# Backward pass of one decode step: two heads' M kept in PSUM, part of wq kept on chip, another order in the third pass

## The chip, the cores and the metric

The kernel runs on one core of a Trainium2 chip. The metric is the device time of one execution in microseconds; the time before is the median of three runs. A profiled execution, recorded apart from those runs, gives the trace. The engines are TensorE (PE, with PEld for its weight loads), VectorE (DVE), ScalarE (ACT), GpSimd (POOL) and SyncE (SP). DMAs are issued by ScalarE, GpSimd and SyncE, each on a queue of its own, and all run on the same 16 DMA engines.

## The reference

The forward pass is one token through attention over a cached window and a gated feed-forward layer; what is asked for is its output and the gradients of everything that goes in:

```python
W = min(4096, max(256, Sk // 4))                      # 4096 of Sk = 32768
q = (layernorm(x) @ wq)                               # 16 heads of 256, 8 K/V heads
scores = einsum("bhqd,bhkd->bhqk", q, k[last W]) * (Dh ** -0.5)
p = softmax(scores); o = einsum("bhqk,bhkd->bhqd", p, v[last W])
h  = x + o @ wo
h2 = h + ((hn @ w_gate) * (hn @ w_up)) @ w_down       # hn = layernorm(h)
_out, _vjp = jax.vjp(_f, x, k_cache, v_cache, wq, wo, w_gate, w_up, w_down)
return (_out, *_vjp(grad_out))
```

All tensors are bf16. x and grad_out have 448 numbers, wq is 448x4096, wo 4096x448, w_gate and w_up 448x1792, w_down 1792x448, and each cache 8 heads x 32768 x 256. The gradients of the two caches (out_2, out_3) are zero outside the last 4096 positions of each head: 28,672 of 32,768 rows of 256 numbers, 235 MB in all, are zeros to be written. The gradient of wq is out_4, of wo out_5, of w_gate and w_up out_6 and out_7, of w_down out_8; out_0 is h2 and out_1 the gradient of x.

## The kernel before

The kernel has a first pass over the 8 K/V heads (forward attention), a middle part (feed-forward, forward and backward, and the gradient of the attention output), and a third pass over the heads, which writes the cache gradients. A scheduler orders the instructions of each engine at build time; each engine then works through its own list in that order and waits where an operand isn't there.

**On-chip memory.** One arena, laid out by hand: offsets are in KB per partition (KB = 512 bf16 elements). S1 to S4 hold 16 KB each, MB is a region of 32 KB, RB one of 52.5 KB, and there are two buffers outside, `home` (16 KB) and `pair` (32 KB). V_of and K_of say where the V and K of each head lie. V of heads 5 and 6 lies in the halves of `pair`, V of head 7 in S2.

**Zero fills.** The zeros of the 16 regions go out on SyncE's queue, issued at L248. Two early ones read a cleared `pair`; the others read 32 cleared rows of `home`, at most two in flight (DEEP). One of them (UNEVEN) is cut into unequal parts.

**First pass** (`scores`, `moments`, the loop over g in which `scores(g+1)` is called before `moments(g)`). For each head, `dots` transposes K on TensorE (L311) and multiplies it with q (L314); after the softmax, `moments` scales K by the probabilities on VectorE (L367) and accumulates on TensorE M, the product of V and the scaled K (L371), and the sums for o (L375). M (128 x 1024 f32 in two PSUM banks) is copied by ScalarE to M_sb (L379), in MB. The first loads are all on SyncE's queue (L121, L122, L209); later K and V are loaded on ScalarE's queue when `NEXT` says, after the head whose slot they take. MB holds wq (wqA 24 KB, wqB 4 KB) until q is computed (L231, L233). K of head 3 is loaded into MB, after that.

**Middle.** wo (L398, L402), w_down (L399) and the gate and up weights (L404, L405) are loaded into RB and beyond. The gradient for o comes from 32 dot products of wo with dh on VectorE (L509) and a product (L514).

**Third pass**, in the head order 3, 1, 4, 5, 0, 6, 2, 7. For each head, `dots` again (V with the gradient of o, on TensorE at L311 and L314, copied by VectorE and ScalarE at L655 and L653), then 16 products (L680) whose results VectorE (L687, L688) and ScalarE (L684, L685) cast to two staging buffers (`stage`), and a pair of stores of 2048 KB each on ScalarE's queue (L690). `plan` adds other jobs to each iteration. `dq_all` computes dq from the eight M (L562 to L570), in the first iteration. `spread_all` writes the rows of the gate and up gradients into `pair` (L408, L412, L413). GpSimd computes the weight gradients: `job_d` (out_8), `job_o` (out_5), `job_g` and `job_gB` (out_6, out_7), `job_q` and `job_qB` (out_4), each into one of two staging buffers `wst` of 12 KB (L580, L609 to L612), and stores them on its own queue (L591, L596, L603, L620, L625, L635). For the gradient of x, wq is loaded again into `pair` (L695, L696, L701) and multiplied with dq on VectorE (L707, L710). V of heads 0 and 2 is brought into S3 (L692, L693, and a load at L209).

Of the kernel before, what the change touches and what calls it, by code (L numbers as in the profile page):

```python
# [8 lines left out]
f32 = mybir.dt.float32  # L9
# [4 lines left out]
D = 448  # L14
# [21 lines left out]
def kernel(  # L36
# [20 lines left out]
    def ar(off, n):  # L57
        return arena[:, off:off + n]
# [16 lines left out]
    KT_slot = [ar(RB + (32 + 2 * i) * KB, 2 * KB) for i in range(3)]  # L75
# [132 lines left out]
    def load_kv(dst, cache, g, queue=LD):  # L208
        queue.dma_start(out=dst, in_=cache[0, g, Sk - W:, :].rearrange("(p t) d -> p t d", t=T))  # L209
# [31 lines left out]

    load_kv(K_of[3], A_k_cache, 3, ZQ)

    def rows_of(src, n):
# [76 lines left out]
    with tc.tile_pool(name="ps_m", bufs=1, space=bass.MemoryType.PSUM) as ps_m, \  # L321
            tc.tile_pool(name="ps_x", bufs=1, space=bass.MemoryType.PSUM) as ps_x, \
            tc.tile_pool(name="ps_c", bufs=1, space=bass.MemoryType.PSUM) as ps_c, \
# [35 lines left out]
        def moments(g, p_f):  # L359
            K_sb, V_sb = K_of[g], V_of[g]  # L360
            M_ps = ps_m.tile([128, 2, 2 * Dh], f32, tag="M")
            for c in range(8):
                pK = pK_slot[c % 2]
                for i in range(4):
                    t = 4 * c + i
                    for hh in range(2):
                        nc.vector.tensor_scalar(out=pK[:, i, hh, :], in0=K_sb[:, t, :], scalar1=p_f[:, 8 * i + c, hh:hh + 1], scalar2=None, op0=ALU.mult)  # L367
                for i in range(4):
                    t = 4 * c + i
                    for vh in range(2):  # L370
                        nc.tensor.matmul(M_ps[:, vh, :], lhsT=V_sb[:, t, vh * 128:(vh + 1) * 128], rhs=pK[:, i, :, :].rearrange("p h d -> p (h d)"),  # L371
                                         start=(t == 0), stop=(t == T - 1))
# [41 lines left out]

    with tc.tile_pool(name="ps_mid", bufs=3, space=bass.MemoryType.PSUM) as ps_mid, \
            tc.tile_pool(name="ps_f", bufs=1, space=bass.MemoryType.PSUM) as ps_f, \
            tc.tile_pool(name="workm", bufs=1) as workm:
# [30 lines left out]
        dhn2 = workm.tile([128, 2, 2, 5], f32)  # L448
        ffn_ps = ps_f.tile([1, D], f32, tag="ffn")

# [103 lines left out]
        LD.dma_start(out=out_0.rearrange("a b d -> (a b) d"), in_=h2_bf)  # L554

    with tc.tile_pool(name="work2", bufs=2) as work2, tc.tile_pool(name="lnw", bufs=1) as lnw, \
            tc.tile_pool(name="ps_d", bufs=2, space=bass.MemoryType.PSUM) as ps_d:
# [13 lines left out]

        HJ = H * Dh // 2
        wst_ctr = [0]
# [20 lines left out]
        def job_d(h):  # L594
            def st(buf):
                nc.gpsimd.dma_start(out=out8_v[h], in_=buf[:, 0:NB * D])  # L596
            return lambda: outer([(dh2_bc[:], hh_f[:, h, b:b + 1], D) for b in range(NB)], st)

        def job_g(i):
# [27 lines left out]

        HJ = H * Dh // 2

        def job_qB():  # L630
# [7 lines left out]
        def spread_all():  # L638
            for i in range(2):
                for q in range(4):  # L640
                    spread_dg(diag3, ps_t, "tmp", i, q, dg_bc[:, i, q * D:(q + 1) * D])

        plan = [[dq_all], [job_d(0), job_d(1)], [job_o(0, 13), job_o(13, 13)], [job_o(26, 6), spread_all, job_g(0)], [job_g(1), job_gB()],
                [job_q(0), job_q(1)], [job_q(2), job_qB()], []]

        stc = 0
        for it, g in enumerate((3, 1, 4, 5, 0, 6, 2, 7)):
            V_sb = kv(S[3]) if g in (0, 2) else V_of[g]
# [45 lines left out]
            if it == 3:  # L694
                LD.dma_start(out=wq2A[:, 0, :], in_=wq_A[:, 0, :])  # L695
                LD.dma_start(out=wq2B, in_=wq_B)  # L696
            if it == 4:
                load_kv(kv(S[3]), A_v_cache, 2)
            if it == 5:
                for c in range(1, 3):  # L700
                    LD.dma_start(out=wq2A[:, c, :], in_=wq_A[:, c, :])  # L701
            for job in plan[it]:
                job()
            if it == 6:
                dn1 = lnw.tile([128, 5], f32)
                for c in range(3):
                    nc.vector.tensor_tensor_reduce(out=wq2A[:, c, :], in0=wq2A[:, c, :], in1=dq_bc, scale=1.0, scalar=0.0,  # L707
                                                   op0=ALU.mult, op1=ALU.add, accum_out=dn1[:, c:c + 1])
                for h in range(2):
                    nc.vector.tensor_tensor_reduce(out=wq2A[:, h, 0:HJ], in0=wq2B, in1=dq_bc[:, h * HJ:(h + 1) * HJ], scale=1.0, scalar=0.0,  # L710
                                                   op0=ALU.mult, op1=ALU.add, accum_out=dn1[:, 3 + h:4 + h])
                dcat1 = lnw.tile([128, 8], f32)
# [39 lines left out]
```

## Time and profile before

| what | value |
|---|---|
| time, median of 3 runs | 789.95 us (789.61 to 789.96) |
| the profiled execution's own time | 789.11 us |
| its span, first to last instruction | 787.3 us |
| mean granted TensorE clock | 0.753 |
| TensorE, VectorE, ScalarE, GpSimd busy | 62%, 50%, 25%, 24% of the span |
| HBM read, written | 52.00 MB, 280.59 MB |

The page of the profile cuts the span into 40 slices (19.7 us each) and gives the busy share of each engine in tenths, the DMA engines' mean share and what they moved. Further views are the busy times by stretch, the waits (engine, line, what it waited for, total, times, longest), the chain of work that ended last, and the timeline of single instructions. A name like `arena<-d_ps` is the written tile and the read one.

### The profile page before, as it was taken

What the parts mean: (1) busy time and instruction counts of PE and PEld (TensorE: products, weight loads), DVE (VectorE), ACT (ScalarE), POOL (GpSimd) and SP (SyncE); (2) the same over time, 40 slices, a digit from 0 to 9 for tenths busy, and PEclk for the clock granted to TensorE, in tenths of its full rate; (3) what the DMA queues carried; (4) which work ended last, traced back from release to release, by engine and by line L of the source; (5) the groups of instructions that cost most, each with busy time, mean ns of one, the idle gap of its engine ahead of it and who ended that gap; (6) DMA issues with size and microseconds to landing.
All of it is one profiled execution on the core that took longest, in us unless ns stands there. A gap on an engine that the chain in (4) does not pass through costs nothing.

```text
span 787.3 us, 6396 instructions
## 1 busy us (share of the span) xinstructions
PE 486.3 (62%) x2184; PEld 205.2 (26%) x2184; DVE 396.0 (50%) x1087; ACT 198.0 (25%) x309; POOL 187.0 (24%) x95
## 2 busy tenths in 40 slices
PE   1999999999699929234043156997528605826230
PEld 1444444434344414011012012342212302302000
DVE  8168536436026614213427845267358219897230
ACT  1351331340430001000001025155315302515230
POOL 7000000000000000000000000595934369494710
PEclk9999999999869959565555567998756855556555
DMA  9999999999999999999999999999999999999996
GB/s 379 430 423 432 433 428 422 420 427 431 430 433 429 426 430 429 427 429 428 429 433 432 433 429 420 431 422 428 418 431 420 430 427 432 431 427 420 429 427 282
DMA packets 23118, 333.01 MB, mean 423 GB/s; under 512 B 1290, under 2 KB 2318, under 8 KB 3694
## 3 DMA queue, kind: packets, MB, share of 16 engines
q1 hardware_dynamic: 15189, 255.33, 76.2%
q10 hardware_dynamic: 5320, 56.56, 17.0%
q0 software_dynamic: 2576, 20.71, 6.3%
q8 instruction: 17, 0.28, 0.1%
q14 instruction: 16, 0.12, 0.0%
HBM read 52.00 MB, written 280.59 MB: 422 GB/s over the span
## 4 chain that ended last, share of the span: by engine, by line
PE 47%; DMA 28%; DVE 16%; issue 4%; ACT 2%; SPq 0%; DVEq 0%; ACTq 0%; POOLq 0%
PE M_ps L371 15%; DMA pair<-in_A_wq_dram 8%; DMA arena<-in_B_w_up_dram 8%; PE tr_ps L311 7%; PE rows_ps L314 7%; PE ok_ps L375 6%; DMA arena<-in_A_k_cache_dram 4%; DMA out_dram<-arena 4%; DMA arena<-in_A_v_cache_dram 3%; DVE arena L509 2%; PE d_ps L680 2%; DVE arena L688 2%; DVE arena L687 2%; PE dqb_ps L562 2%; DMA arena<-in_B_w_down_dram 2%
## 5 line engine op out<-in xcount | busy, mean ns | idle before, releaser
L367 DVE TENSOR_SCALAR arena<-arena,p_f 128x256 bf16<-128x256 bf16 x512 | 110.2, 280 | 56.1 <-PE M_ps L371 53.5
L311 PE MATMUL tr_ps<-ident_f,arena 128*128 128x128 f32 x448 | 87.0, 324 | 35.1 <-DMA arena<-in_A_k_cache_dram 21.4
L680 PE MATMUL d_ps<-arena 32*128 32x512 bf16 x256 | 49.4, 515 | 78.5 <-DVE arena L688 67.0
L314 PE MATMUL rows_ps<-arena,vpad 128*16 128x512 bf16 x256 | 89.6, 449 | 9.2 <-ACT arena L653 3.2
L371 PE MATMUL M_ps<-arena 128*128 128x512 bf16 x320 | 78.1, 390 | 16.5 <-DMA arena<-in_A_v_cache_dram 15.2
L328 ACT COPY arena<-tr_ps 128x1024 bf16<-128x1024 bf16 x64 | 63.7, 1013 | 90.3 <-PE tr_ps L311 77.5
L311 PEld LDWEIGHTS tr_ps<-ident_f,arena 128*128 128x128 f32 x448 | 56.4, 161 | 113.8 <-issue 81.0
L687 DVE CAST arena<-d_ps 128x512 bf16<-128x512 f32 x64 | 47.3, 750 | 29.1 <-PE d_ps L680 26.6
L684 ACT CAST arena<-d_ps 128x512 bf16<-128x512 f32 x64 | 38.0, 593 | 93.8 <-PE d_ps L680 87.4
L688 DVE CAST arena<-d_ps 128x512 bf16<-128x512 f32 x64 | 46.8, 742 | 9.5 <-DMA out_dram<-arena 9.5
L653 ACT COPY arena<-tr_ps 128x1024 bf16<-128x1024 bf16 x32 | 32.8, 1028 | 61.8 <-PE rows_ps L314 36.3
L580 POOL TENSOR_SCALAR arena<-dh_bc,oX_f 128x448 bf16<-128x448 bf16 x32 | 44.4, 1398 | 10.8 <-DMA out_dram<-arena 9.9
L371 PEld LDWEIGHTS <-arena 128*128 128x128 bf16 x320 | 30.5, 101 | 53.6 <-DMA arena<-in_A_v_cache_dram 17.3
L375 PE MATMUL ok_ps<-arena 128*32 128x512 bf16 x208 | 43.3, 380 | 0.0
L402 POOL DMA_DIRECT2D arena<-in_A_wo_dram x1 | 0.5, 528 | 179.9 <-PE ok_ps L375 179.9
L685 ACT CAST arena<-d_ps 128x512 bf16<-128x512 f32 x64 | 38.4, 600 | 16.0 <-DMA out_dram<-arena 16.0
L580 POOL TENSOR_SCALAR arena<-pair,xT 128x1792 bf16<-128x1792 bf16 x6 | 35.8, 5978 | 23.4 <-ACT pair L413 23.4
L680 PEld LDWEIGHTS <-arena 32*128 32x128 bf16 x256 | 11.0, 96 | 115.8 <-DVE arena L688 80.2
L707 DVE CUSTOM_DVE_ANT_0 pair<-pair,arena 128x4096 bf16<-128x4096 bf16 x3 | 18.2, 6070 | 40.2 <-DMA pair<-in_A_wq_dram 40.2
L580 POOL TENSOR_SCALAR arena<-arena,xT 128x4096 bf16<-128x4096 bf16 x3 | 31.8, 10612 | 23.3 <-DMA out_dram<-arena 23.3
L379 ACT COPY arena<-M_ps 128x512 f32<-128x512 f32 x16 | 8.6, 589 | 100.4 <-PE M_ps L371 100.4
L316 DVE COPY arena<-rows_ps 16x512 f32<-16x512 f32 x16 | 10.8, 676 | 43.3 <-PE rows_ps L314 43.1
(235 smaller groups left out, 616.0 us busy)
## 6 DMA issues: line engine op xcount, KB each, us to landing
out_dram<-home SPq DMA_DIRECT2D x13, 14336.0 KB, 83.9
out_dram<-arena ACTq DMA_DIRECT2D x16, 2048.0 KB, 25.3
out_dram<-pair SPq DMA_DIRECT2D x2, 14336.0 KB, 79.7
out_dram<-home SPq DMA_DIRECT2D x1, 12288.0 KB
arena<-in_A_k_cache_dram SPq DMA_DIRECT2D x4, 2048.0 KB, 22.0
arena<-in_A_k_cache_dram ACTq DMA_DIRECT2D x4, 2048.0 KB, 20.2
arena<-in_A_v_cache_dram SPq DMA_DIRECT2D x3, 2048.0 KB, 28.4
arena<-in_A_v_cache_dram ACTq DMA_DIRECT2D x3, 2048.0 KB, 24.3
```

The costliest lines, as they stand in the source:

```text
L311: nc.tensor.transpose(tr_ps[:, i, :], X_sb[:, 4 * q + i, :].bitcast(f32), ident_f[:])
L314: nc.tensor.matmul(rows_ps[:], lhsT=pad[:, e, 16 * q:16 * q + 16], rhs=XT.rearrange("p (n e) -> p n e", e=2)[:, :, e], start=(q == 0 and e ...
L328: sT_ps = dots(K_of[g], KT_slot, vpad[g % 2], rows1, ps_c, "cols", lambda q, XT, ps: nc.scalar.copy(out=XT, in_=ps))
L367: nc.vector.tensor_scalar(out=pK[:, i, hh, :], in0=K_sb[:, t, :], scalar1=p_f[:, 8 * i + c, hh:hh + 1], scalar2=None, op0=ALU.mult)
L371: nc.tensor.matmul(M_ps[:, vh, :], lhsT=V_sb[:, t, vh * 128:(vh + 1) * 128], rhs=pK[:, i, :, :].rearrange("p h d -> p (h d)"), start=(t == ...
L375: nc.tensor.matmul(ok_ps[32 * k:32 * (k + 1), :], lhsT=ppad[g % 2][:, t:t + 2, :].rearrange("p t h -> p (t h)"), rhs=X_sb[:, t:t + 2, :].r ...
L580: nc.gpsimd.tensor_scalar(out=buf[:, off:off + n], in0=src, scalar1=col, scalar2=None, op0=ALU.mult)
L680: nc.tensor.matmul(d_ps[:, qi].rearrange("p w d -> p (w d)"), lhsT=rm[32 * q:32 * (q + 1), l, :], rhs=Rs[32 * q:32 * (q + 1), :], start=Tr ...
L684: nc.scalar.copy(out=stV[:, t:t + 2, :], in_=d_ps[:, :, 0, :])
L685: nc.scalar.copy(out=stK[:, t:t + 2, :], in_=d_ps[:, :, 1, :])
L687: nc.vector.tensor_copy(out=stV[:, t:t + 2, :], in_=d_ps[:, :, 0, :])
L688: nc.vector.tensor_copy(out=stK[:, t:t + 2, :], in_=d_ps[:, :, 1, :])
```

## The change

- wqA and wqB lie 4 KB further up in MB, M_sb of heads 6 and 7 lies at RB, and the two `wst` buffers have 8 KB each. So the second half of wq's third block (4 KB) and wqB (4 KB) are not overwritten.
- M of heads 6 and 7 is not copied in the first pass: head 6 stays in its PSUM tile, head 7 is accumulated in the two transpose buffers (`ps_tr`), and both are copied after the wo dots. The pool of M stays open until then; the middle's pool has two banks instead of three, and the feed-forward sum is in the bank of `rows`.
- K of heads 3 to 7 lies in other slots, K of head 3 is loaded on ScalarE's queue after head 0, and `NEXT` has other entries (V of head 7 after head 5 instead of 6).
- `dq_all` is called ahead of the third pass, whose head order is 3, 1, 4, 6, 5, 0, 7, 2.
- The jobs are cut and planned differently; the third row block of out_6 and out_7 has its own job (`job_g2`).
- wq is reloaded as two blocks of 1024 KB and a half of 512 KB, and its dots with dq are one more.

```diff
-    K_of = [kv(o) for o in (RB, RB + 16 * KB, S[4], MB + 16 * KB, RB, RB + 16 * KB, S[2], RB)]
+    K_of = [kv(o) for o in (RB + 16 * KB, RB, S[4], RB + 16 * KB, RB, S[2], RB + 16 * KB, RB)]
-    M_sb = [ar(MB + 4 * KB * g, 4 * KB).bitcast(f32).rearrange("p (v h d) -> p v h d", v=2, h=2) for g in range(G)]
-    wqA = ar(MB, 24 * KB).rearrange("p (c j) -> p c j", c=3)
-    wqB = ar(MB + 24 * KB, 4 * KB)
+    M_sb = [ar(o, 4 * KB).bitcast(f32).rearrange("p (v h d) -> p v h d", v=2, h=2)
+            for o in [MB + 4 * KB * g for g in range(6)] + [RB, RB + 4 * KB]]
+    wqA = ar(MB + 4 * KB, 24 * KB).rearrange("p (c j) -> p c j", c=3)
+    wqB = ar(MB + 28 * KB, 4 * KB)
...
-    dg_bc = pair[:, 0:2 * F].rearrange("p (i f) -> p i f", i=2)
+    dg_bc = pair[:, ZW:ZW + 2 * F].rearrange("p (i f) -> p i f", i=2)
-    wst = [ar(MB + (8 + 12 * i) * KB, 12 * KB) for i in range(2)]
-    wq2A = pair[:, 8 * KB:32 * KB].rearrange("p (c j) -> p c j", c=3)
-    wq2B = ar(P3 + 33 * KB // 2, 4 * KB)
+    wst = [ar(MB + (8 + 8 * i) * KB, 8 * KB) for i in range(2)]
+    HJ = H * Dh // 2
+    wq2 = [pair[:, 0:2 * HJ], pair[:, 2 * HJ:4 * HJ], pair[:, ZW + 4 * KB + 2 * HJ:ZW + 4 * KB + 3 * HJ], wqA[:, 2, HJ:2 * HJ]]
...
-    load_kv(K_of[3], A_k_cache, 3, ZQ)
...
+    def move_M(g, M_ps):
+        for vh in range(2):
+            nc.scalar.copy(out=M_sb[g][:, vh].rearrange("p h d -> p (h d)"), in_=M_ps[vh])
...
-            M_ps = ps_m.tile([128, 2, 2 * Dh], f32, tag="M")
+            if g < G - 1:
+                M_t = ps_m.tile([128, 2, 2 * Dh], f32, tag="M", name="M_t")
+                M_ps = [M_t[:, vh, :] for vh in range(2)]
+            else:
+                M_ps = [ps_tr.tile([128, 4, 128], f32, tag="tr", name="M_t")[:].rearrange("p t k -> p (t k)") for _ in range(2)]
...
-            for vh in range(2):
-                nc.scalar.copy(out=M_sb[g][:, vh].rearrange("p h d -> p (h d)"), in_=M_ps[:, vh, :])
-        NEXT = {0: ((0, 4),), 1: ((0, 5),), 2: ((1, 4), (0, 6)), 4: ((0, 7),), 6: ((1, 7),)}
+            if g < G - 2:
+                move_M(g, M_ps)
+            else:
+                M_late.append((g, M_ps))
+        NEXT = {0: ((0, 3),), 1: ((0, 4),), 2: ((0, 5), (1, 4)), 3: ((0, 6),), 4: ((0, 7),), 5: ((1, 7),)}
...
-    with tc.tile_pool(name="ps_mid", bufs=3, space=bass.MemoryType.PSUM) as ps_mid, \
-            tc.tile_pool(name="ps_f", bufs=1, space=bass.MemoryType.PSUM) as ps_f, \
+    with tc.tile_pool(name="ps_mid", bufs=2, space=bass.MemoryType.PSUM) as ps_mid, \
...
-        ffn_ps = ps_f.tile([1, D], f32, tag="ffn")
+        ffn_ps = ps_s.tile([1, D], f32, tag="rows")
...
+        for g, M_ps in M_late:
+            move_M(g, M_ps)
...
         def job_g(i):
-            ov = (out_6, out_7)[i]
             def st(buf):
-                nc.gpsimd.dma_start(out=ov[0:384, :].rearrange("(p c) f -> p (c f)", c=3), in_=buf[:, 0:3 * F])
-            return lambda: outer([(dg_bc[:, i, :], hnT_f[:, c:c + 1], F) for c in range(3)], st)
+                nc.gpsimd.dma_start(out=out67[i][:, 0:2 * F], in_=buf[:, 0:2 * F])
+            return lambda: outer([(dg_bc[:, i, :], hnT_f[:, c:c + 1], F) for c in range(2)], st)
+        def job_g2():
+            def st(buf):
+                for i in range(2):
+                    nc.gpsimd.dma_start(out=out67[i][:, 2 * F:], in_=buf[:, i * F:(i + 1) * F])
+            return lambda: outer([(dg_bc[:, i, :], hnT_f[:, 2:3], F) for i in range(2)], st)
...
-        plan = [[dq_all], [job_d(0), job_d(1)], [job_o(0, 13), job_o(13, 13)], [job_o(26, 6), spread_all, job_g(0)], [job_g(1), job_gB()],
+        plan = [[job_d(0), job_d(1)], [job_o(0, 9), job_o(9, 9)], [job_o(18, 9), job_o(27, 5)], [spread_all, job_g(0), job_g(1)], [job_g2(), job_gB()],
                 [job_q(0), job_q(1)], [job_q(2), job_qB()], []]
+        dq_all()
-        for it, g in enumerate((3, 1, 4, 5, 0, 6, 2, 7)):
+        for it, g in enumerate((3, 1, 4, 6, 5, 0, 7, 2)):
...
             if it == 3:
-                LD.dma_start(out=wq2A[:, 0, :], in_=wq_A[:, 0, :])
-                LD.dma_start(out=wq2B, in_=wq_B)
+                LD.dma_start(out=wq2[2], in_=wq_A[:, 2, 0:HJ])
             if it == 4:
+                for c in range(2):
+                    LD.dma_start(out=wq2[c], in_=wq_A[:, c, :])
+            if it == 5:
                 load_kv(kv(S[3]), A_v_cache, 2)
-            if it == 5:
-                for c in range(1, 3):
-                    LD.dma_start(out=wq2A[:, c, :], in_=wq_A[:, c, :])
...
             if it == 6:
-                dn1 = lnw.tile([128, 5], f32)
-                for c in range(3):
-                    nc.vector.tensor_tensor_reduce(out=wq2A[:, c, :], in0=wq2A[:, c, :], in1=dq_bc, ...)
-                for h in range(2):
-                    nc.vector.tensor_tensor_reduce(out=wq2A[:, h, 0:HJ], in0=wq2B, in1=dq_bc[:, h * HJ:(h + 1) * HJ], ...)
+                dn1 = lnw.tile([128, 6], f32)
+                for c, src, dq in ((0, wq2[0], dq_bc), (1, wq2[1], dq_bc), (2, wq2[2], dq_bc[:, 0:HJ]), (5, wq2[3], dq_bc[:, HJ:2 * HJ]),
+                                   (3, wqB, dq_bc[:, 0:HJ]), (4, wqB, dq_bc[:, HJ:2 * HJ])):
+                    nc.vector.tensor_tensor_reduce(out=wq2[0][:, 0:src.shape[1]], in0=src, in1=dq, ...)
+                nc.vector.tensor_tensor(out=dn1[:, 2:3], in0=dn1[:, 2:3], in1=dn1[:, 5:6], op=ALU.add)
```

More of the change, by code (lines that the diff above doesn't have):

```diff
@@ L320, in dots @@
         return cols_ps
-    with tc.tile_pool(name="ps_m", bufs=1, space=bass.MemoryType.PSUM) as ps_m, \
-            tc.tile_pool(name="ps_x", bufs=1, space=bass.MemoryType.PSUM) as ps_x, \
+    ps_m_cm = tc.tile_pool(name="ps_m", bufs=1, space=bass.MemoryType.PSUM)
+    ps_m = ps_m_cm.__enter__()
+    M_late = []
+    with tc.tile_pool(name="ps_x", bufs=1, space=bass.MemoryType.PSUM) as ps_x, \
             tc.tile_pool(name="ps_c", bufs=1, space=bass.MemoryType.PSUM) as ps_c, \
@@ L370, in moments @@
                     for vh in range(2):
-                        nc.tensor.matmul(M_ps[:, vh, :], lhsT=V_sb[:, t, vh * 128:(vh + 1) * 128], rhs=pK[:, i, :, :].rearrange("p h d -> p (h d)"),
+                        nc.tensor.matmul(M_ps[vh], lhsT=V_sb[:, t, vh * 128:(vh + 1) * 128], rhs=pK[:, i, :, :].rearrange("p h d -> p (h d)"),
                                          start=(t == 0), stop=(t == T - 1))
@@ L554 @@
         LD.dma_start(out=out_0.rearrange("a b d -> (a b) d"), in_=h2_bf)
+    ps_m_cm.__exit__(None, None, None)
     with tc.tile_pool(name="work2", bufs=2) as work2, tc.tile_pool(name="lnw", bufs=1) as lnw, \
@@ L570, in dq_all @@
                 nc.scalar.activation(out=dq_bc[:, g * 512:(g + 1) * 512], in_=dqb_ps[:, 1, :], func=ACT.Copy, scale=SCALE)
-        HJ = H * Dh // 2
         wst_ctr = [0]
@@ L597, in job_d @@
             return lambda: outer([(dh2_bc[:], hh_f[:, h, b:b + 1], D) for b in range(NB)], st)
+        out67 = [o[0:384, :].rearrange("(p c) f -> p (c f)", c=3) for o in (out_6, out_7)]
         def job_g(i):
-            ov = (out_6, out_7)[i]
             def st(buf):
-                nc.gpsimd.dma_start(out=ov[0:384, :].rearrange("(p c) f -> p (c f)", c=3), in_=buf[:, 0:3 * F])
-            return lambda: outer([(dg_bc[:, i, :], hnT_f[:, c:c + 1], F) for c in range(3)], st)
+                nc.gpsimd.dma_start(out=out67[i][:, 0:2 * F], in_=buf[:, 0:2 * F])
[5 more added lines that the diff above has]
+            return lambda: outer([(dg_bc[:, i, :], hnT_f[:, 2:3], F) for i in range(2)], st)
         def outer_B(buf, off, src, xT, n):
@@ L626, in job_q @@
             return lambda: outer([(dq_bc, xnT_f[:, c:c + 1], H * Dh)], st)
-        HJ = H * Dh // 2
         def job_qB():
@@ L704 @@
             if it == 6:
-                dn1 = lnw.tile([128, 5], f32)
-                for c in range(3):
-                    nc.vector.tensor_tensor_reduce(out=wq2A[:, c, :], in0=wq2A[:, c, :], in1=dq_bc, scale=1.0, scalar=0.0,
+                dn1 = lnw.tile([128, 6], f32)
+                for c, src, dq in ((0, wq2[0], dq_bc), (1, wq2[1], dq_bc), (2, wq2[2], dq_bc[:, 0:HJ]), (5, wq2[3], dq_bc[:, HJ:2 * HJ]),
+                                   (3, wqB, dq_bc[:, 0:HJ]), (4, wqB, dq_bc[:, HJ:2 * HJ])):
+                    nc.vector.tensor_tensor_reduce(out=wq2[0][:, 0:src.shape[1]], in0=src, in1=dq, scale=1.0, scalar=0.0,
                                                    op0=ALU.mult, op1=ALU.add, accum_out=dn1[:, c:c + 1])
-                for h in range(2):
-                    nc.vector.tensor_tensor_reduce(out=wq2A[:, h, 0:HJ], in0=wq2B, in1=dq_bc[:, h * HJ:(h + 1) * HJ], scale=1.0, scalar=0.0,
-                                                   op0=ALU.mult, op1=ALU.add, accum_out=dn1[:, 3 + h:4 + h])
+                nc.vector.tensor_tensor(out=dn1[:, 2:3], in0=dn1[:, 2:3], in1=dn1[:, 5:6], op=ALU.add)
                 dcat1 = lnw.tile([128, 8], f32)
```

## The prediction

> **What bounds the kernel now.** First the page's slices and DMA totals, which say whether any engine can matter at all.
>
> ```profile
> DMA  9999999999999999999999999999999999999996
> GB/s 379 430 423 432 433 428 422 420 427 431 430 433 429 426 430 429 427 429 428 429 433 432 433 429 420 431 422 428 418 431 420 430 427 432 431 427 420 429 427 282
> DMA packets 23118, 333.01 MB, mean 423 GB/s; under 512 B 1290, under 2 KB 2318, under 8 KB 3694
> ...
> q1 hardware_dynamic: 15189, 255.33, 76.2%
> q10 hardware_dynamic: 5320, 56.56, 17.0%
> q0 software_dynamic: 2576, 20.71, 6.3%
> ```
>
> The 16 DMA engines are busy in every slice but the last. q1 is SyncE's queue (the zero fills, which can nearly always run), q10 ScalarE's, q0 GpSimd's. So the time is bytes over rate, and a stall of an engine costs nothing while fills are left. Where that cover ends is in the busy times by stretch (last columns: DMA share, GB/s):
>
> ```profile
> 758.00:762.00 4.00, 0.83 (x4) 0.10 (x1) 1.29 (x2) 1.25 (x3) 0.00 (x0) 0.50 1.00 423
> 776.00:778.00 2.00, 0.00 (x0) 0.00 (x0) 0.00 (x0) 0.00 (x0) 0.00 (x0) 0.50 0.94 401
> 784.00:786.00 2.00, 0.00 (x0) 0.00 (x0) 0.00 (x0) 0.00 (x0) 0.00 (x0) 0.50 0.14 57
> ```
>
> Compute is over at 760, the DMA engines stay full to 777 and finish one by one to 786. Two chains of stores run under that cover, ScalarE's (a pair per head) and GpSimd's (weight gradients). The timeline has the last links of both:
>
> ```profile
> 602.07 14.35 POOL L580 TENSOR_SCALAR arena<-pair,xT 128x1792 bf16<-128x1792 bf16 x3 [23.39 <-ACT pair L413]
> ...
> 705.67 1.14 POOL L625 DMA_DIRECT2D out_dram<-arena  x2
> ...
> 734.03 5.43 POOL L609 TENSOR_SCALAR arena<-arena,XB 128x2048 bf16<-128x2048 bf16 x1 [4.16 <-DMA out_dram<-arena]
> ...
> 749.92 0.62 POOL L635 DMA_DIRECT2D out_dram<-arena  x1 [0.30 <-POOL arena L612]
> ```
>
> ```profile
> 759.49 1.65 ACTq L690 DMA_DIRECT2D out_dram<-arena  x2
> ```
>
> GpSimd starts the gate gradients at 602, when ScalarE has written the gate rows (L413), and needs 148 us to its last store; before the last job it waits for a staging buffer until 734, 27 us after that buffer's store was issued. Last, the chain, for where VectorE is held, and with it everything behind it:
>
> ```profile
> 274.48 15.16 DMA arena<-in_A_v_cache_dram
> 544.56 32.77 DMA pair<-in_A_wq_dram
> 615.18 30.58 DMA pair<-in_A_wq_dram
> ```
>
> **Part 1: DMA work.** wq is reloaded as 2.5 MB instead of 3.5: -1.05 MB, at 428 GB/s 2.45 us. The smaller buffers cut stores into shorter rows. By the trace's single packets (10,752 bytes 404 ns, 3,584 bytes 145 ns, and 7,168 at the 26.3 GB/s an engine that their neighbours show, 272 ns) out_6 and out_7 cost (272+145-404) x 256 / 16 engines = 0.2 us more, out_5 by the same reckoning 0.1; the two extra DMAs' 4-byte packets, 9 ns each, nothing. Sum -2.2: the work alone would end the span at 787.3-2.2 = 785.1.
>
> **Part 2: up to the third pass.** K3's load leaves SyncE's queue (where it and the fills behind it waited 19.0 us for the q product) and goes out after head 0, at 72.3; with the 20.2 us of such loads it lands at 93, needed at 102.8. K4 to K6 go out one head later and are needed no sooner than their slots' old tenants (K4: 123 against 133). V7 goes out when head 5 is done (254.4) instead of head 6, so the 15.2 us go. But wo and w_down now go out after head 6 with the gate weights behind them: 2.3 MB at half of 428 GB/s, 11 us, most of it beside head 7: net -12 (-15 to 0). Four copies of M (589 ns) move behind the tenth wo dot; head 7's M holds both transpose buffers until then, and VectorE's order after the change has two evictions of V3's transposes among the dots: +3 (0 to 6). One mid bank less: 0 to 2, I take 1, as weight loads set that chain. The wo gradient's product (449.3) comes near 441.
>
> **Part 3: the third pass.** Its store pairs are issued at 490.0, 537.7, 560.1, 606.7, 680.1, 715.7, 732.3 and 759.5 in the timeline of before. dq (490.9 to 518.3 in the chain, 27.5 us; twice that if all at clock 0.5) now precedes the first pair: 490-8+27.5 = 509. The second pair writes a buffer that the first store must leave (15.5 us at least, more beside GpSimd's stores, which start earlier as their 47.6 us wait for dq shrinks), then takes 16 to 20 us: 545 (530 to 550).
>
> Now the reload. By VectorE's order after the change, the first 4096-wide wq dot stands ahead of the last evictions of the third pair, one pair earlier than before. Its load is issued near the pair's end, behind the second pair in ScalarE's queue: the chain had it landed 39 us after the pair ahead (538.3 to 577.3), with GpSimd quieter I take 36: 581; dot 4.4 us and evictions: third pair 588. The second wq load stands behind that pair: another 32 to 39 us, 588+33 = 621, dot to 625. Behind this dot stand the spreads that write the gate rows, the fourth of them after four eviction steps (2 us each): GpSimd's gate rows are ready near **636** (625 to 646) instead of 602. The fourth pair comes near 660 (606.7 before), but later pairs need no wq and are paced by their queue: pairs four and five with V2's load between are 10.5 MB at 214 GB/s, 49 us; seventh near 730, eighth near **760**, as before.
>
> GpSimd from 636, with two buffers of 8 KB: gate job 2 x 6.0 us; its store must land (16 us, by 13.7 to 18.6 of 1344 KB) before the third row block, 6; three more ops 18; their store 16; B rows 9.4; q job 10.6; rest of the B rows 6.5; wait for the q job's store (18.0 us from issue), 14.6 left; two q jobs back to back 21.2, and only then, by GpSimd's order, both their stores. With four issues of 0.6 us that is 133 us: 769, against 706 before. The last job (15.9 us, 734.0 to 749.9) fills the buffer of the second of these stores. Before, that one landed 27 us after issue; here the DMA work is through near 784, so 784 (bounds: 5 us of bytes, 774; 27 us, 796). That makes the end insensitive: with the stores issued anywhere from 757 to 779, 22 us, the second lands near 784. Then 784+16 = 800 for the last store, 0.5 MB, 1.2 us of bytes and about 2 of latency: span **803**. Nothing lies beside this: the fills are done.
>
> **Sum.** The profiled execution took 789.1, 1.8 around its span; the runs' median is 0.84 above it. 803+1.8+0.84 = 805.6. The second pair at 530 would bring all forward by 15 us, of which the landing leaves 3; the early side is the wider one, so I say **805 us**.
>
> **Rivals.** (a) *DMA-bound, faster.* If GpSimd's last store is issued by 777, only the bytes count: 789.1+0.84-2.2 = 787.7. With 16 us for the last job and 18 to 27 for the landing, that needs the two q stores at 734 to 743, 26 to 35 us before my reckoning: for it, shorter waits if ScalarE's queue is less shared; against it, the order on VectorE, which puts both wq dots ahead of the spreads, and that the early end of the gate rows (625) gives only 11 of those microseconds. (b) *No change,* 788.4 to 791.4: the last store between 777 and 784. (c) *ScalarE's last pair late.* If dq runs at half clock throughout (+27) the eighth pair is issued near 785 instead of 760; alone it needs 9.8 us for 4.19 MB and 2 more, span 797, but the same delay also moves GpSimd's q stores to 796, landing 5 later, and its last store to 817: span 820, 823 us. It decides once the q stores leave after 779. (d) *The V7 gain isn't there:* 12 us later, q stores at 781, landing 786: span 805, 808 us.
>
> (e) *Stores land fast.* A mechanism for (a): once fills run out, a store takes bytes plus latency. If all four buffer waits (61 us) were so, some 45 us would go and (a) would hold. The rows against it: 1024 KB takes 18.0 us, 224 KB 13.6, as every packet queues beside fills up to the end. The Trainium skill, page "DMA: Bandwidth & Descriptors", section "Anatomy of one DMA", gives a GpSimd DMA 2.0 us plus its bytes at 436 GB/s; by that, an estimate, a 1024 KB store takes 4.4 us and the time would be 787.7. The trace does not agree while the queues are full.
>
> **How the numbers follow.** Forecast with (d): 0.67, own range 797 to 811. (c): 0.06. (a) with (e): 0.17. (b): 0.07; the rest of 0.03 lies beyond. The range reaches down to (a), whose chance is too large to leave out beside (c), and stops short of (c): **787.5 to 812**. About 0.2% (1.6 us) is what can be told from no change: faster 0.18, within 0.07, slower 0.75.
>
> **What would show it.** DMA total 331.96 MB, HBM read 50.95; no TensorE wait for V near 274; VectorE's wait for wq, 40.2 us now, in two waits on successive pairs, both before GpSimd's first gate op, which comes near 636; GpSimd's last store near 800, after the eighth pair (760); a last stretch of about 15 us with the DMA engines nearly idle. Wrong: gate rows before 612, or the DMA engines full up to the last 10 us.

## The result, and the profile after

The changed kernel takes 792.37 us (median of 22 runs, 787.79 to 795.98) against 789.87 (22 runs, 789.61 to 790.35) of the kernel before in the same session: ratio 1.003, 95% interval 1.0018 to 1.0041. It is slower, by 2.5 us, where 15 were forecast. The profiled execution took 791.51 us with a span of 789.7.

The page's slices and DMA totals of the changed kernel, beside those shown for before:

```profile
DMA  9999999999999999999999999999999999999994
GB/s 380 427 429 427 430 430 423 421 429 431 430 431 430 430 425 431 428 429 430 433 427 435 427 433 418 426 428 426 418 430 432 428 417 425 436 423 427 424 429 180
DMA packets 23277, 331.96 MB, mean 420 GB/s; under 512 B 1321, under 2 KB 2349, under 8 KB 4493
...
q1 hardware_dynamic: 15045, 253.23, 75.3%
q10 hardware_dynamic: 5320, 57.61, 17.3%
q0 software_dynamic: 2880, 20.71, 6.3%
```

There are 1.05 MB less to move (333.01 before), and the engines are as full as before in every slice but the last, which fell from 282 to 180 GB/s. So the loss is in the last 20 us. The busy times by stretch there (the columns before the last two are the engines' busy times, TensorE to GpSimd, and TensorE's clock; the last two are DMA share and GB/s):

```profile
772.00:776.00 4.00, 0.00 (x0) 0.00 (x0) 0.00 (x0) 0.00 (x0) 4.00 (x2) 0.50 0.89 381
776.00:780.00 4.00, 0.00 (x0) 0.00 (x0) 0.00 (x0) 0.00 (x0) 4.00 (x1) 0.50 0.32 135
780.00:784.00 4.00, 0.00 (x0) 0.00 (x0) 0.00 (x0) 0.00 (x0) 3.92 (x2) 0.50 0.09 37
784.00:788.00 4.00, 0.00 (x0) 0.00 (x0) 0.00 (x0) 0.00 (x0) 1.26 (x2) 0.50 0.32 131
```

The DMA engines have little left from 776 on and nothing at 784, while GpSimd still computes, and then they move one more store. Before, they were full to 777 and ended at 786 with nothing on GpSimd. Its timeline in the changed kernel, from the gate rows on:

```profile
613.42 9.58 POOL L593 TENSOR_SCALAR arena<-pair,xT 128x1792 bf16<-128x1792 bf16 x2 [80.63 <-ACT pair L424]
...
740.40 1.15 POOL L644 DMA_DIRECT2D out_dram<-arena  x2
769.67 5.43 POOL L628 TENSOR_SCALAR arena<-arena,XB 128x2048 bf16<-128x2048 bf16 x1 [28.13 <-DMA out_dram<-arena]
...
784.95 0.61 POOL L652 DMA_DIRECT2D out_dram<-arena  x1 [0.30 <-POOL arena L631]
```

The gate jobs start at 613.4 (602.1 before). The two q stores leave at 740.4 and 741.0, and the last job, the B rows of out_4, waits 28.1 us, until the second has left its staging buffer. Its own store leaves at 785. The end of the chain of waits says the same:

```profile
741.00 28.58 DMA out_dram<-arena
769.58 0.09 issue
769.67 5.43 POOL arena L628
775.10 5.43 POOL arena L630
780.53 0.07 issue
780.61 4.05 POOL arena L631
784.65 0.27 issue
784.92 0.64 POOLq L763
```

ScalarE's last pair is no part of it: in the changed kernel it is issued at 735.8, 24 us earlier than before (759.5).

```profile
735.77 1.64 ACTq L708 DMA_DIRECT2D out_dram<-arena  x2
```

So the third pass ends earlier, fewer bytes are moved, and still the end is later, because the buffer for GpSimd's last job comes free only at 769.6.

### The profile page after: what moved, and what is told of

Its sections match the earlier page's. It is cut to its first block, busy times and chain, and to the rows that moved or that the text cites. A ratio compares the mean times of both kernels' runs of the same rounds, so it can differ in the third digit from the quotient of the medians.

```text
span 789.7 us, 6400 instructions
## 1 busy us (share of the span) xinstructions
PE 482.4 (61%) x2184; PEld 205.4 (26%) x2184; DVE 382.1 (48%) x1090; ACT 198.3 (25%) x309; POOL 182.2 (23%) x98
## 2 busy tenths in 40 slices
DMA packets 23277, 331.96 MB, mean 420 GB/s; under 512 B 1321, under 2 KB 2349, under 8 KB 4493
## 3 DMA queue, kind: packets, MB, share of 16 engines
q10 hardware_dynamic: 5320, 57.61, 17.3%
HBM read 50.96 MB, written 280.59 MB: 420 GB/s over the span
## 4 chain that ended last, share of the span: by engine, by line
PE 43%; DMA 30%; DVE 11%; POOL 9%; another core or an unknown queue 2%; issue 2%; ACT 2%; SPq 0%; POOLq 0%; ACTq 0%; DVEq 0%
PE M_t L380 13%; DMA out_dram<-arena 10%; PE rows_ps L317 7%; PE tr_ps L314 6%; DMA arena<-in_A_v_cache_dram 6%; PE ok_ps L384 6%; DMA pair<-in_A_wq_dram 5%; POOL arena L593 5%; DMA arena<-in_A_k_cache_dram 4%; DVE arena L519 2%; DMA arena<-in_A_wo_dram 2%; PE dqb_ps L576 2%; DMA arena<-in_B_w_down_dram 2%; DMA arena<-in_B_w_up_dram 1%
## 5 line engine op out<-in xcount | busy, mean ns | idle before, releaser
L698 PE MATMUL d_ps<-arena 32*128 32x512 bf16 x256 | 47.7, 519 | 77.5 <-DVE arena L706 67.6
L380 PE MATMUL M_t<-arena 128*128 128x512 bf16 x320 | 75.4, 380 | 2.2 <-DMA arena<-in_A_v_cache_dram 2.2
L705 DVE CAST arena<-d_ps 128x512 bf16<-128x512 f32 x64 | 44.2, 690 | 37.8 <-PE d_ps L698 37.5
L706 DVE CAST arena<-d_ps 128x512 bf16<-128x512 f32 x64 | 43.7, 683 | 16.2 <-DMA out_dram<-arena 16.2
L593 POOL TENSOR_SCALAR arena<-pair,xT 128x1792 bf16<-128x1792 bf16 x6 | 28.7, 4795 | 98.3 <-ACT pair L424 80.6
L671 ACT COPY arena<-tr_ps 128x1024 bf16<-128x1024 bf16 x32 | 32.6, 1024 | 42.6 <-PE rows_ps L317 25.9
L593 POOL TENSOR_SCALAR arena<-arena,xT 128x4096 bf16<-128x4096 bf16 x3 | 31.8, 10616 | 17.3 <-DMA out_dram<-arena 17.3
L473 PE MATMUL r_ps<-arena,X2pad 128*4 128x448 bf16 x24 | 10.4, 572 | 38.8 <-DMA arena<-in_B_w_up_dram 23.2
L317 PEld LDWEIGHTS <-vpad 128*16 128x16 bf16 x256 | 18.2, 93 | 51.3 <-issue 46.0
```

The costliest lines, as they stand in the source:

```text
L380: nc.tensor.matmul(M_ps[vh], lhsT=V_sb[:, t, vh * 128:(vh + 1) * 128], rhs=pK[:, i, :, :].rearrange("p h d -> p (h d)"), start=(t == 0), s ...
L593: nc.gpsimd.tensor_scalar(out=buf[:, off:off + n], in0=src, scalar1=col, scalar2=None, op0=ALU.mult)
L698: nc.tensor.matmul(d_ps[:, qi].rearrange("p w d -> p (w d)"), lhsT=rm[32 * q:32 * (q + 1), l, :], rhs=Rs[32 * q:32 * (q + 1), :], start=Tr ...
L705: nc.vector.tensor_copy(out=stV[:, t:t + 2, :], in_=d_ps[:, :, 0, :])
L706: nc.vector.tensor_copy(out=stK[:, t:t + 2, :], in_=d_ps[:, :, 1, :])
```

## The experiments

All ran beside the kernel before; its medians in the three sessions were 789.84, 789.76 and 790.00 us. Each can be read against the changed kernel's 792.37 and against 787.7, rival (a)'s time if only the bytes count. The four numbers of the table come from each version's profiled execution; the time is the median.

| version | gate jobs start | q stores issued | last store issued | span | time |
|---|---|---|---|---|---|
| changed kernel | 613.4 | 740.4 | 785.0 | 789.7 | 792.37 |
| last job in areas of its own | 614.7 | 743.2 | 754.3 | 786.3 | 787.75 |
| spreads earlier | 587.2 | 716.5 | 762.8 | 785.9 | 787.65 |
| all of wq reloaded | 607.8 | 734.2 | 779.3 | 788.3 | 790.15 |
| GpSimd delayed | 614.5, idle work among them | 760.3 | 798.4 | 803.2 | 804.94 |
| dq later | 610.8 | 737.3 | 782.1 | 786.9 | 789.26 |
| dots without the reload | 583.3 | 707.3 | 753.4 | 786.1 | 787.62 |
| V7 later | 621.6 | 749.9 | 793.2 | 798.0 | 797.05 |
| delayed, own areas | 613.3, idle work among them | 758.9 | 770.0 | 785.8 | 787.65 |
| own areas and spreads earlier | 585.4 | 711.8 | 722.8 | 786.0 | 787.75 |

**Is it the wait for the staging buffer?** The last job gets an idle part of `pair` and, as a new argument of `outer_B`, the idle dq rows:

```diff
...
-                buf = wst[wst_ctr[0] % 2]
-                wst_ctr[0] += 1
-                outer_B(buf, 0, dq_bc, xnT_f, HJ)
-                nc.gpsimd.dma_start(out=out4_B, in_=buf[:, 0:HJ])
+                buf = pair[:, ZW + 8 * KB:ZW + 12 * KB]
+                outer_B(buf, 0, dq_bc, xnT_f, HJ, ar(P3 + 33 * KB // 2, 4 * KB))
+                nc.gpsimd.dma_start(out=out4_B, in_=buf)
```

> The changed kernel, with GpSimd's last job (q gradient, B rows) written into two idle areas of its own instead of the staging buffer that the second q store still reads. Theory (GpSimd's chain of stores sets the end, through the 28.1 us wait of its last job): that job starts at 741 instead of 769.7, its store is issued near 757, the DMA engines stay full to the end and only the bytes count: 789.9 - 2.2 = 787.7 us. Rival (the DMA engines' own tail, or ScalarE's pairs, set the end and the late store only fills a gap): 792.4, unchanged.

Measured 787.75 us (787.27 to 789.28), ratio 0.9977 (0.9968 to 0.9985). GpSimd's timeline of this version:

```profile
743.22 1.14 POOL L645 DMA_DIRECT2D out_dram<-arena  x2
744.39 5.45 POOL L631 TENSOR_SCALAR arena<-arena,XB 128x2048 bf16<-128x2048 bf16 x1
749.92 4.05 POOL L632 TENSOR_TENSOR pair<-pair,arena 128x2048 bf16<-128x2048 bf16 x1
754.26 0.61 POOL L652 DMA_DIRECT2D out_dram<-pair  x1 [0.30 <-POOL pair L632]
```

The q stores leave 3 us later than in the changed kernel and the last store 31 us earlier; nothing stands in the brackets but the 0.3 us of an issue. Without the wait the change is 2 us faster instead of 2.5 us slower. (The scheduler also placed the job's first operation, 5.45 us, at 705.3, in a wait ahead of the q jobs. So the 31 us are the wait of 28 and this operation, less the 3 by which the q stores are later.) The theory's number (787.7) is met, the rival falls.

**Is it when the gate rows are ready?** The spreads stand ahead of the fourth pair's evictions:

```diff
+            if it == 3:
+                spread_all()
             stV, stK = stage[stc], stage[stc + 1]
...
-[spread_all, job_g(0), job_g(1)]
+[job_g(0), job_g(1)]
```

> The changed kernel, with the spreads that write the gate rows placed ahead of the fourth pair's evictions, so that on VectorE the four of the first gate stand ahead of the second wq dot (they stood behind it). Theory (when the gate rows are ready decides, through GpSimd's chain of 127 us): gate rows near 590 instead of 613.4, q stores near 718, last store near 762, before the DMA work is through: 787.7 us. A rival in which the end is not tied to the gate rows: 792.4. One in which the spreads ahead of the evictions hold ScalarE's pairs up: later than 792.

Measured 787.65 us (787.22 to 788.28), ratio 0.9972 (0.9962 to 0.9983). Lines of its GpSimd timeline:

```profile
587.20 9.58 POOL L593 TENSOR_SCALAR arena<-pair,xT 128x1792 bf16<-128x1792 bf16 x2 [54.97 <-ACT pair L424]
...
747.51 5.43 POOL L628 TENSOR_SCALAR arena<-arena,XB 128x2048 bf16<-128x2048 bf16 x1 [29.84 <-DMA out_dram<-arena]
...
762.79 0.61 POOL L652 DMA_DIRECT2D out_dram<-arena  x1 [0.30 <-POOL arena L631]
```

The last job waits as long as in the changed kernel (29.8 us), but 22 us earlier, where the DMA engines are full: the same wait costs nothing. So it's the wait and its place together. One correction to the expectation: in the changed kernel not all four spreads of the first gate stood behind the second wq dot, but only the last one (VectorE has the others at 491.1, 580.5 and 587.3, the dot at 603.7). The edit moves that one.

**Do the bytes count?** All 3.5 MB of wq are loaded again, into areas that are idle, and the dots read them there:

```diff
...
                 LD.dma_start(out=wq2[2], in_=wq_A[:, 2, 0:HJ])
+                LD.dma_start(out=wq2[3], in_=wq_A[:, 2, HJ:2 * HJ])
+                LD.dma_start(out=wq2B, in_=wq_B)
```

> The changed kernel with all 3.5 MB of wq loaded a second time, as before the change (the last third's second half and the B rows into idle areas): 1.05 MB more, two loads more in ScalarE's queue. Theory (the end hangs on GpSimd's chain, not on bytes): 792 to 793.5, as the second q store lands a little later; DMA total 333.0 MB. Rival (bytes set the end): 792.4 + 2.45 = 794.8.

Measured 790.15 us (789.90 to 792.05): neither. It is *faster* than the changed kernel with 1.05 MB more to move. Its VectorE order is another one: three of the four spreads of the first gate stand ahead of its first 4096-wide dot (one does in the changed kernel), and it has one wait for wq instead of two. The gate jobs start 5.7 us earlier, and the last store leaves at 779.3, while the engines still have work (share 0.36 from 778 to 780). The two lines, from GpSimd's timeline and from the waits (total, times, longest):

```profile
607.75 9.58 POOL L594 TENSOR_SCALAR arena<-pair,xT 128x1792 bf16<-128x1792 bf16 x2 [77.22 <-ACT pair L425]
```

```profile
DVE pair L728 <- DMA pair<-in_A_wq_dram: 30.6, 1, 30.6
```

So this version is limited by its bytes, or nearly: by the trace's packets SyncE's queue ends at 785.1 and GpSimd's last store at 786.2. Against the versions that are limited by their bytes (787.65) it is 2.5 us longer, which is what 1.05 MB were priced at (2.45), though up to 1 us of it may be the late store's. The expectation failed in taking the gate rows as unmoved by an edit of the loads.

**What if the gate rows came as late as forecast?** Five idle operations among GpSimd's gate jobs:

```diff
+            if i == 0:
+                def run():
+                    for _ in range(5):
+                        nc.gpsimd.tensor_scalar(out=pair[:, ZW + 8 * KB:ZW + 8 * KB + F], in0=dg_bc[:, 0, :], scalar1=hnT_f[:, 0:1], ...)
+                    outer([(dg_bc[:, i, :], hnT_f[:, c:c + 1], F) for c in range(2)], st)
+                return run
```

> The changed kernel with five idle GpSimd operations of 4.8 us (128x1792, written to an area that nothing reads) ahead of its first gate job: its chain starts near 637 instead of 613.4, as the prediction had it. Theory as predicted (the two q stores go out near 764, and the second lands when the DMA work is through, near 784): last job 784 to 800, 803 us or so (801 to 807). If that store takes 28 us from issue whatever is in the queues: 792.5, last store at 808, 812.5 us. A pure shift: 792.4 + 24 = 816. If GpSimd's chain doesn't set the end: 792.4.

Measured 804.94 us (803.80 to 805.27), ratio 1.0186 (1.0172 to 1.02).

```profile
760.26 1.15 POOL L650 DMA_DIRECT2D out_dram<-arena  x2
783.16 5.43 POOL L634 TENSOR_SCALAR arena<-arena,XB 128x2048 bf16<-128x2048 bf16 x1 [21.75 <-DMA out_dram<-arena]
...
798.44 0.61 POOL L658 DMA_DIRECT2D out_dram<-arena  x1 [0.30 <-POOL arena L637]
```

The scheduler wove the idle operations into the first gate jobs, so that 24 us of work became a delay of 20 at the q stores (740.4 to 760.3). The second store still lands as the engines run dry, at 783, after 21.8 us instead of 28.1. A delay of 20 us costs 13.5 at the last store (785.0 to 798.4) and 12.6 in the time.

**And is it lateness, or the wait?** The delay and the last job's own areas in one kernel:

> The delayed kernel (804.94: GpSimd's chain starts 24 us later) with the last job in two areas of its own, as in the first experiment. Theory (not the lateness but the wait for the staging buffer costs the time): q stores near 761 as in the delayed kernel, the last job straight behind them, its store issued near 772 to 776, while the DMA engines are still full; 787.7 to 789 us. Rival (a chain that starts this late sets the end with or without the buffer): 800 to 805.

Measured 787.65 us (787.56 to 788.23), ratio 0.9972 (0.9961 to 0.9982): 17.3 us less than with the delay alone, by another place for one 512 KB result.

```profile
758.94 1.14 POOL L651 DMA_DIRECT2D out_dram<-arena  x2
760.10 5.45 POOL L637 TENSOR_SCALAR arena<-arena,XB 128x2048 bf16<-128x2048 bf16 x1
765.64 4.04 POOL L638 TENSOR_TENSOR pair<-pair,arena 128x2048 bf16<-128x2048 bf16 x1
769.98 0.61 POOL L658 DMA_DIRECT2D out_dram<-pair  x1 [0.30 <-POOL pair L638]
```

**What holds the gate rows?** In this kernel the dots read the part of wq that stays on chip:

```diff
-                for c, src, dq in ((0, wq2[0], dq_bc), (1, wq2[1], dq_bc), ...
...
+                for c in (0, 0, 1, 1, 2, 5, 3, 4):
+                    nc.vector.tensor_tensor_reduce(out=jk, in0=wqB, in1=dq_bc[:, 0:HJ], ...)
```

> The changed kernel with eight half-width dots on the part of wq that stays on chip in place of the dots on the reloaded part (the loads are still made, nothing reads them; the normalization's gradient of x is not the reference's). VectorE's two waits for wq, 30.6 us, are gone. Theory (the gate rows stand behind those waits): gate rows near 583 (613.4 - 30.6; 575 to 595), last store before 765, 787.7 us. Rival (the gate rows are held by ScalarE's evictions and the d_ps banks, not by VectorE's wait): gate rows within 8 us of 613, 791 to 792.4 us.

Measured 787.62 us (787.28 to 788.54), ratio 0.9974 (0.9963 to 0.9984). GpSimd's first gate job:

```profile
583.30 9.91 POOL L593 TENSOR_SCALAR arena<-pair,xT 128x1792 bf16<-128x1792 bf16 x2 [47.38 <-ACT pair L424]
```

583 was expected: VectorE's 30.6 us of waiting for wq are gone, and the gate rows come 30.1 us earlier. So they hang on that wait. That the two numbers agree so closely is in part chance, as the dots now stand elsewhere on VectorE (538 to 570) and the third pair leaves 7 us later (562.8).

**Is dq's new place paid for?** dq behind the first pair, as before. In this kernel the first pair's staging overwrites M of heads 6 and 7, so their columns of out_4, and what follows from them, are not the reference's.

```diff
-        dq_all()
-        plan = [[job_d(0), job_d(1)], ...
+        plan = [[dq_all, job_d(0), job_d(1)], ...
```

> The changed kernel with the query gradient (dq, 24 us of it) put back behind the first head's evictions, as before the change. Theory (the gate rows' time decides, and dq ahead of the first pair delays all pairs): first pair near 475 to 480 instead of 498.9, the second paced by its store's landing, gate rows 5 to 20 us earlier than 613.4 and the time with them: 787.7 to 789.5. Rival (dq's place is hidden by the buffer wait of the second pair, which the prediction priced at -8 + 27.5 + 36): 792.4, gate rows unchanged within 3 us.

Measured 789.26 us (787.64 to 793.33), ratio 1.0001 (0.9989 to 1.0013). The pairs of the two kernels, changed kernel first, then this one (ScalarE's DMA issues):

```profile
498.86 1.65 ACTq L708 DMA_DIRECT2D out_dram<-arena  x2
531.53 1.65 ACTq L708 DMA_DIRECT2D out_dram<-arena  x2
555.59 1.68 ACTq L708 DMA_DIRECT2D out_dram<-arena  x2
```

```profile
474.63 1.64 ACTq L707 DMA_DIRECT2D out_dram<-arena  x2
522.37 1.77 ACTq L707 DMA_DIRECT2D out_dram<-arena  x2
545.16 1.63 ACTq L707 DMA_DIRECT2D out_dram<-arena  x2
```

The first pair is 24.2 us earlier, the second 9.2, the third 10.4, and the gate rows 2.6 (613.4 to 610.8): both waits for wq are longer here, 35.7 us together instead of 30.6. By the gate rows the rival holds, by the time the theory, though the time lies just above the point where the last store is early enough, where 3 us decide. Either way, dq's place explains about 3 us.

**Is the earlier V7 load a gain?** A one-element copy holds the load of V7 until head 6's M is there:

```diff
-        NEXT = {..., 4: ((0, 7),), 5: ((1, 7),)}
+        NEXT = {..., 4: ((0, 7),), 6: ((1, 7),)}
...
+            if g == G - 2:
+                nc.scalar.copy(out=V_of[7][:, 0, 0:1], in_=M_late[0][1][0][:, 0:1])
```

> The changed kernel with V7's load held by a one-element copy until head 6's moments are done (near 275 instead of 254.8), which undoes the earlier V7 load alone; wo and w_down stand behind it. Theory (the gain of V7, -12 in the prediction, is carried to the gate rows and from there to the end): the wo gradient's product at 447 to 453 instead of 435.1, gate rows 12 to 18 us later, last job after a store that lands near 782, last store 797: 799 to 804 us. Rival (the gain is swallowed by a later wait, on wq or on a staging buffer): the product later but gate rows within 5 us of 613 and 792 to 794 us.

Measured 797.05 us (792.69 to 800.61; the profiled execution is one of its longer ones), ratio 1.0092 (1.0062 to 1.0123), below the expected 799 to 804. TensorE and GpSimd in this version:

```profile
284.98 1.44 PE L380 MATMUL M_t<-arena 128*128 128x512 bf16 x3 [9.92 <-DMA arena<-in_A_v_cache_dram]
...
443.85 1.04 PE L528 MATMUL do_ps<-arena,ET_f 128*16 128x256 f32 x2 [11.68 <-DVE arena L525]
```

```profile
749.87 1.15 POOL L646 DMA_DIRECT2D out_dram<-arena  x2
777.97 5.42 POOL L630 TENSOR_SCALAR arena<-arena,XB 128x2048 bf16<-128x2048 bf16 x1 [26.95 <-DMA out_dram<-arena]
```

The load was held to 269.1 only (274.5 before the change), so the wait that came back is 9.9 us, not 15. In the profiled executions it is carried on almost whole: product 8.8 us later, gate jobs 8.1, q stores 9.5, last store 8.3 (785.0 to 793.2). By the medians of the time it is 4.7. The rival, a gain swallowed on the way, falls; the size expected was too large, as the load was held less long than thought.

**Is there anything left?** Both cures in one kernel, and two other ways to share out the 30 extra rows of the uneven fill:

> Both cures together: the earlier spreads (787.65) and the last job's own areas (787.75). Theory (each alone already leaves only the bytes, so there is nothing left for the second): 787.4 to 788.0. Rival (GpSimd's late store still costs something at the end in either of them): below 787.0.

> The version with the spreads placed earlier (787.65), with the 30 extra rows of the uneven zero fill written from 15 partitions in 2 rows each instead of 3 partitions in 10. In that version about five of the sixteen DMA engines work on alone from 778 to 782. Theory (engines with extra rows end last): the tail gets shorter, 784 to 786.5 us. Rival (the extra rows balance something else, so that others end later without them): 787.7 to 791.

> The version with earlier spreads, the 30 extra rows of the uneven fill from 6 partitions in 5 rows each (3 x 10 gave 787.65, 15 x 2 gave 788.74). Theory (the extra rows balance engines that other transfers load less, and 3 x 10 is near the best): between, 787.6 to 788.7. Rival (three engines are given too much, and half as much is the balance): 786 to 787.3.

Both cures: 787.75 us (787.38 to 788.12), with the last store at 722.8 instead of 754 to 763. Nothing is gained below the bytes. The rows as 15 x 2 take 788.74 (788.53 to 789.30), inside the rival's range; as 6 x 5 790.59 (790.17 to 790.87), above both ranges given. So 3 x 10 (787.65) is the best of the three, and the extra rows do balance something; what, stays open, since the profile has the DMA engines' mean only.

## Why the prediction was right or wrong

**The mechanism.** Right in these links: GpSimd's two-buffer chain takes over the end, its last job waits for the buffer of the second q store, and the engines run dry meanwhile. Another place for that job's results, which takes the wait away, gives 787.75 against the 787.7 of rival (a).

**The step that failed** is "GpSimd's gate rows are ready near 636 (625 to 646)", from the third pair's place in VectorE's order. They were ready at 613.4, outside the range given for them and just above the bound of 612 that was named as a sign of being wrong. VectorE's two waits in the changed kernel, and the work between:

```profile
574.97 4.43 DVE L725 CUSTOM_DVE_ANT_0 pair<-pair,arena 128x4096 bf16<-128x4096 bf16 x1 [14.87 <-DMA pair<-in_A_wq_dram]
...
587.31 0.62 DVE L419 TENSOR_TENSOR arena<-ident_f,dgu_f 128x448 bf16<-128x448 f32 x1
603.70 4.42 DVE L725 CUSTOM_DVE_ANT_0 pair<-pair,arena 128x4096 bf16<-128x4096 bf16 x1 [15.78 <-DMA pair<-in_A_wq_dram]
...
610.45 0.61 DVE L419 TENSOR_TENSOR arena<-ident_f,dgu_f 128x448 bf16<-128x448 f32 x1
```

The prediction had the first dot ahead of the last evictions of the *third* pair, and so the third pair at 588. The trace has that pair's stores at 555.6, 19 us before this dot; the evictions behind the dot are the fourth pair's. With the third pair gone, the second wq load could be issued at 560.9. ScalarE's issue of it, and its writes of the third and the fourth spread, the last one just ahead of the gate jobs:

```profile
560.85 0.35 ACTq L716 DMA_DIRECT2D pair<-in_A_wq_dram  x1
...
590.21 0.60 ACT L424 CAST pair<-bc_ps 128x448 bf16<-128x448 f32 x1
...
612.76 0.55 ACT L424 CAST pair<-bc_ps 128x448 bf16<-128x448 f32 x1
```

In the prediction's own terms the 22.6 us are made up like this. The third pair left at 555.6 instead of 588: 32.4 us earlier. The second dot, waiting for its load, started 48.1 us after that pair (603.7), where 33 were put: 15.1 back; what made the load so long, no run shows. The dot was 0.4 longer. And from its end (608.1) to the gate jobs it was 5.3 us instead of 11, since only the fourth of the spreads stood behind it: 5.7. With 613.4 in place of 636, and the rest of its sum left as it was (133, the 27 us named as a bound for the landing, 16, 3.2 and 2.6), the prediction would have said 795 us. This is read from one trace; no run moves the third pair alone.

**The rest of the working** ran as forecast when the gate rows' lateness was supplied by hand. With the q stores 20 us later, the second of them landed at 783 (forecast "near 784", wherever between 757 and 779 it was issued), the last store left at 798.4 (800), the span was 803.2 (803) and the time 804.94 (805). The insensitivity has an edge, though, to which the prediction gave too little weight: a store issued at 741 takes its 28 us in the queue and lands at 769.6. There the end follows the gate rows nearly one to one, as the version with V7 later shows (q stores at 750; gate jobs 8.1 us later, last store 8.3).

**Part 1.** 331.96 MB and 50.96 MB read, as worked out; -2.2 us was forecast and -2.1 measured where the chain is out of the way (787.75 against 789.84).

**Part 2.** V7: head 7's products start at 274.8, 14.9 us earlier than before (289.7), with -12 forecast for the load; the wo gradient's product comes at 435.1, 14.2 us earlier than before, where +4 was booked for the copies of M and the missing bank. Between the two places 0.7 us of the gain were lost. Right in kind, 6 us too late in sum.

**Part 3.** dq, at a granted clock of 1.00 from 442 to 466, took 24 us, not 27.5; the second pair came at 531.5, not 545. From the gate rows to the q stores the chain took 127 us, not 133: its six 128x1792 operations took 4.8 us each, where 6.0, the mean before, was put. The last store is listed with 3.0 us to landing; 3.2 was forecast.

**Rivals.** (a), limited by the bytes: the changed kernel's q stores at 740.4 lie inside the 734 to 743 named for it, but the buffer took 28 us, past the 18 to 27 reckoned, and the last store left at 785, not by 777. Five versions of the experiments are there, at 787.62 to 787.75. (b) is what came closest in time, 788.4 to 791.4 against 792.4, with the last store 1 us past its bound of 784. (c) and (d) did not occur: ScalarE's last pair came at 735.8, and the V7 gain was there.

(e), fast landing. On empty DMA engines it is so, under the fills it isn't:

```profile
out_dram<-arena POOLq DMA_DIRECT2D x3, 1024.0 KB, 20.7
...
out_dram<-arena POOLq DMA_DIRECT2D x1, 512.0 KB, 3.0
```

(The changed kernel's DMA issues: KB each, median us to landing.) The rule of the Trainium skill, page "DMA: Bandwidth & Descriptors", section "Anatomy of one DMA", 2.0 us plus the bytes at 436 GB/s, gives 3.2 us for 512 KB, an estimate. The trace agrees for the one store that had the engines to itself, and has 20.7 us where the rule gives 4.4 for 1024 KB.

## What to carry to other kernels

Under a transfer-bound kernel the end can hang on one staging buffer: work back from the point where the DMA engines run dry, through the landing of the store that the last job's buffer waits for, and give that last job a buffer that nothing else uses. With the engines empty near 784, a wait of 22 to 30 us cost nothing where it ended at 747.5 (spreads earlier), 4.7 us where it ended at 769.7 (the changed kernel) and 17.3 where it ended at 783.2 (the delayed kernel); and a saving of bytes moves that point closer. When the forecast hangs on where one instruction stands in another engine's order, match its neighbours to their head or tile first: one pair was put 32 us too late here, and a load that was put 15 us too short hid half of it.

## What the runs showed of the hardware that was not expected

**Two stores in one queue.** The second of two 1024 KB stores issued 0.6 us apart on GpSimd's queue landed 28 us after issue while the other queues were busy. By the trace's packets their bytes began to move at 745.4, 5 us after the first issue, and the two landed at 758.3 and 769.2: 81 GB/s for the first store, in 12.9 us, and 96 for the second, in 10.9. From 745.4 to 758.3 each of the three queues moved 144 packets, but they carried 2.36 MB on SyncE's queue, 2.10 on ScalarE's and 1.06 on GpSimd's, whose rows have 8 KB where the others' have 16. So in this stretch the queues took equal turns, and a queue's share went by the size of its rows. ScalarE's queue was empty from 766.4 on. The Trainium skill, page "DMA: Bandwidth & Descriptors", section "Queues, rings and completion order", has each DMA engine go round the queues that have work and take a whole packet, there a bundle of several descriptors, from each. If a turn takes equally many rows of 16, 16 and 8 KB, GpSimd gets a fifth of 428 GB/s, 86, or 12.2 us for 1024 KB, an estimate. The trace's 12.9 us for the first store agrees.

**Spread of the runs.** Versions limited by their bytes repeat within 2.2 us (789.90 to 792.05, the widest, with all of wq reloaded), the delayed one within 1.5, but the changed kernel within 8.2, over more runs, and the version with V7 later within 7.9. That fits an end that follows every small shift of a long chain of waits in the one, and is pinned to the moment when the engines run dry in the other; since only one execution of each was profiled, it is not shown.
